# More matmuls on zeros at the start, and a shorter ScalarE program behind the last branch, in an attention and two-expert-layer kernel

## The chip, the cores and the metric

The kernel runs on one core of a Trainium2 chip, in one launch. The time is the device time of that launch in microseconds, from a handful of runs, of which the median counts. One further execution was profiled; its trace has a span (from the first to the last instruction) and the program's own time, which is a little longer.

The core has five engines that run side by side, each with its own instruction stream: TensorE (PE, with its weight loads as PEld), VectorE (DVE), ScalarE (ACT), GpSimd (POOL) and SyncE (SP, which here mostly issues DMA transfers).

## The reference, cut to what matters

Three layers follow each other. All is fp32; q, k, p are drawn eight times larger than the usual 0.1.

```python
# attention through 32 packed queries per head: q, k, v are (4, 8, 576, 64), p is (4, 8, 32, 64)
def sm_attn(qq, kk, vv):
    s = scale * qq @ kk.T;  a = exp(s - max(s));  a = a / (sum(a) + 1e-9);  return a @ vv
p_packed = sm_attn(p, k, v)
x = sm_attn(q, p_packed, p_packed)          # -> (2304, 512)

# first mixture: top-1 expert of 8 with a capacity of 2 * 2304 / 8 tokens
logits = x @ w_gate;  e = argmax(logits);  g = softmax(logits)[e]
keep a token while its expert has had fewer than `capacity`
x = g * (relu(x @ w1[e]) @ w2[e])           # w1 (8, 512, 1024), w2 (8, 1024, 512); zero where not kept

# second mixture: top-1 expert of 8, no capacity, and a sigmoid output gate
e = argmax(x @ w_gate2)
out = softmax(x @ w_gate2)[e] * sigmoid(x @ w_output_gate)[e] * (relu(x @ w1b[e]) @ w2b[e])
```

## The kernel before

The work is done per batch of 576 tokens. All four batches go through the attention; then the kernel looks at which experts the tokens chose and computes, as "slots", only those pairs of batch and expert that hold kept tokens. With the inputs given, two slots are enough. They are written out straight. What other inputs could need (two more slots, and a general path that loops over all experts) stands behind branches at the very end: `rest` is read from memory into a register of every engine (`values_load`, L1101), and `tc.If(rest > 0)` (L1102) skips all of it where nothing is left. With these inputs it is skipped: each engine reads the flag, takes the branch, and goes on to the waits that end the program (shown under L1102 and L1139, the line of `moe.close()` being the last of the function).

Matrix products in fp32 precision are made from split operands: a rounded copy "h" (ScalarE, a `Copy` or `Relu` activation) and the remainder "l" (VectorE, sometimes GpSimd), and three products hh, hl, lh. The functions `high`, `x_high`, `moe1_ppw`, `layer1`, `y_out`, `g2_l` and `moe2_layer2` each hold one such ScalarE instruction.

The order of the work up to the end of the first slot is written out by hand in `PLAN`: a list of steps that are recorded one after the other, each putting its instructions at the end of the streams of the engines it uses. `k00` loads the first third of batch 0's k (one DMA on SP's queue), `tk00` transposes that third on TensorE (six 128x128 transposes, tile `tp`, L25) and copies the result out of PSUM on ScalarE (tile `T`, L265), `p0`/`dup0`/`pT0` do the same for p, `sa00` makes the first scores (tile `s`), and `warm9` issues nine matmuls of a 128x256 block of zeros (`wz`, cleared by VectorE's first instruction, L103), whose result nobody reads:

```python
def warm(n):
    ps = psm("warm")
    for _ in range(n):
        mm(nc, ps[:, 0, 0:256], wz[:, 0:128], wz, True, True)
```

`psm` hands out the four PSUM tiles in turn; a tile is written again when its last reader four tiles earlier is done. The kernel's last useful instructions are in `moe2_layer2` with `last=True`: the last 128 rows of output are made in two halves of 256 columns, each scaled on ScalarE (L751) and sent by a DMA that ScalarE itself issues (L752).

Of the kernel before, what the change touches and what calls it, by code (L numbers as in the profile page):

```python
# [12 lines left out]
ACTF = mybir.ActivationFunctionType  # L13
ALU = mybir.AluOpType
# [11 lines left out]


PLAN = """
k00 hn0 tk00 k01 tk01 warm9 p0 dup0 k10 k02 tk10 tk02 pT0 k11 tk11 k12 p1 v00 q00 q01 tk12 sa00 k20 sa01 dup1 pT1 sa10
sa11 ma00 ea00 cst0 ma01 ea01 ma10 q02 dup2 ma11 cst1 warm7 ea10 at00D v01 at01D ea11 rs1 cap tq00 v02 tq01 tq02 k21  # L30
k22 pp00 v11 pp01 rs0 sc0A tk20 pT2 pt0 tk21 dup3 sb01 tr01 sb00 mb01 tk22 v12 at10 at11 tr00 su01 eb01 mb00 sa20 ma20
sa21 v10 gg0 v22 q10 sm01 q11 pp10 pp11 sc1 ea20 q12 su00 eb00 sm00 tq10 k32 k30 pt1A mu01 v32 tq11 tq12 pT3 warm4
ma21 k31 ea21 bk01 mu00 sb11 q20 bk00 lg01 tr11 mb11 at20D xh0 su11 at21 lt01 tk30 q21 tk31 tk32 eb11 oa01 ob0 rk01
kp01 q22 v20 v21 sb10 tr10 q30 tq20 q31 cn01 tq21 tq22 ei sm11 mu11 rs2 pp20 pp21 wa00 mb10 wa01 wa03 sa30 gg1 sa31
ma30 sc2A v31 pt2 ea30 ma31 tq30 ea31 v30 bk11 sb21 tr21 xl0 mb21 su21 at30 su10 tq31 at31D gg2 w00 sb20 tr20 mb20 w01
h01 q32 eb21 sm21 wb00 rs3 mu21 h00 su20 h03 pp30 eb10 wb01 sm10 pp31 sc3A w03 bk21 mu10 bk10 tq32 pt3A h02 sb30 tr30
sb31 tr31 mb31 wa02 cst3 cl wh00 h06 w02 wl00 eb20 sm20 gg3 mb30 su31 eb31 h07 wh01 sm31 mu20 wb03 bk20 y000 y001 wb02
su30 mu31 eb30 sm30 bk31 h04 h05 y002 y010 y011 y012 mu30 bk30 lg14 cr y013 wl01 lt14 wh03 y003 y004 y005 y006 oa14D
ob1 rk14 wh02 wl02D y014 y015 cst2 kp14 cn14 rt si wl03D y020 wa11 y007 prep y021 y030 wa10 y016 y022 y023 y024 yo00
wa13 y025 y026 y027 wb10 y017 yo01 y031 yo02 y032 y033 y034 xh1 xl1D y035 rr w11 w10 wb11 wa12 y036 y037 yo03 hn1 h13  # L40
zo3 h12 wh10 wl10D h11 h10 w13 w12 gl0 wb12 h14 wh12 gt h17 h15 wh11 wl11 h16 wb13 wh13 wl13D gs gi wl12D zo2
"""


# [1 line left out]
def tile_kernel(  # L46
# [16 lines left out]
    nc = tc.nc  # L63
# [33 lines left out]
        return ps_p.tile([128, 2, 512], FP32, tag="ps", name=name)  # L97

    dma_in = nc.sync.dma_start


    wz = const.tile([128, 256], BF16, name="wz")
# [444 lines left out]
    def high(src, nm, i):  # L547

        hi = (mp["ws2"] if i == 3 else mp["ws"]).tile([128, 1024], FP32R, tag="w", name=nm + "h")
        nc.scalar.activation(out=hi, in_=src.rearrange("p a b -> p (a b)"), func=ACTF.Copy)  # L550
        return hi.rearrange("p (a b) -> p a b", a=src.shape[1])

    def low(src, hi, nm, i, eng):
# [11 lines left out]
    def half(ap):  # L565
        return ap.rearrange("p (u n) -> p u n", u=2)
# [26 lines left out]

    def x_high(a2):
        xh = xs_p.tile([128, 2, S], FP32R, tag="xh", name="xh")
        nc.scalar.activation(out=xh, in_=a2, func=ACTF.Copy)
        return xh

    def x_low(a2, xh, eng):
# [17 lines left out]
    def moe1_ppw(pt, w):  # L617
        ps = ppw_mm(pt, w)
        wh = ppw_p.tile([128, 2, 256], FP32R, tag="wh", name="wh")
        wl = ppw_p.tile([128, 2, 256], FP32R, tag="wl", name="wl")  # L620
        nc.scalar.activation(out=wh, in_=ps[:, :, 0:256], func=ACTF.Copy)
        nc.vector.tensor_tensor(wl, ps[:, :, 0:256], wh.bitcast(FP32), op=ALU.subtract)
        return wh, wl

# [6 lines left out]
    def layer1(h, f, w, x, n, last_first=False):  # L631

        ps = psm("h")
        fs = slice((f % 2) * 128, (f % 2) * 128 + 128)
        chain(ps, [(w[i][:, c, fs], x[j][:, c, :]) for c in range(n) for i, j in ((0, 0), (0, 1), (1, 0))])
        hi = half(h[0][:, f, :])
        nc.scalar.activation(out=hi, in_=ps[:, :, 0:HS], func=ACTF.Relu)  # L637
        lo = h[1][:, f, :]
        cut = HS - LAST
        parts = [(half(lo), ps[:, :, 0:HS], hi)] if not last_first else [  # L640
            (lo[:, 0:HS], ps[:, 0, 0:HS], hi[:, 0]), (lo[:, HS:], ps[:, 1, 0:cut], hi[:, 1, 0:cut]),
            (h[2][:, f, S:S + LAST], ps[:, 1, cut:HS], hi[:, 1, cut:])]
        for o, i, a in parts:
            nc.vector.scalar_tensor_tensor(o, i, 0.0, a.bitcast(FP32), op0=ALU.max, op1=ALU.subtract)  # L644
# [7 lines left out]
                   kk == 0 and x == 0, kk == NF - 1 and x == 2)  # L652

    def y_out(ps, c, y):
        nc.scalar.activation(out=half(y[0][:, c, :]), in_=ps[:, :, 0:HS], func=ACTF.Copy)  # L655
        nc.vector.tensor_tensor(
            half(y[1][:, c, :]), ps[:, :, 0:HS], half(y[0][:, c, :]).bitcast(FP32), op=ALU.subtract)

# [10 lines left out]
    def g2_l(y):  # L669

        lp = psm("l2")
        chain(lp, [(wg2s[:, c, :], y[j][:, c, :]) for c in range(NC) for j in range(2)])
        nc.scalar.activation(out=half(lgT[:4 * E, 0:S]), in_=lp[:4 * E, :, 0:HS], func=ACTF.Copy)

    def g2_t(g1s, slot):
        tp = psm("lt2")
# [56 lines left out]
    def moe2_layer2(h, ws, t, g2, bsel, last=False):  # L733

        n = 128 if t < NT - 1 else LAST
        cs = slice(t * 128, t * 128 + n)
        ps = psm("o")
        o = mp["o"].tile([128, DM], FP32, tag="osb", name="osb")
        parts = ((0, 0), (1, 0), (0, 1))
        if n > 64:  # L740

            w = DM // 2 if last else DM
            seq = [(kk, i, j) for kk in range(NF) for i, j in parts]
            for u in range(DM // w):
                ds_ = slice(u * w, u * w + w)
                if u == 1:
                    ps = psm("o")
                for x, (kk, i, j) in enumerate(seq):
                    mm(nc, ps[:n, 0, 0:w], h[i][:, kk, cs], ws[kk // 2][j][:, kk % 2, ds_], x == 0, x == len(seq) - 1)
                if last:  # L750
                    nc.scalar.activation(out=o[:n, ds_], in_=ps[:n, 0, 0:w], func=ACTF.Copy, scale=g2[:n, t:t + 1])  # L751
                    nc.scalar.dma_start(  # L752
                        out.rearrange("(b s) d -> b s d", b=B)[bass.ds(bsel, 1), t * 128:t * 128 + n, ds_].rearrange(
                            "o s d -> (o s) d"), o[:n, ds_])
            if last:
                return
            nc.scalar.activation(out=o[:n], in_=ps[:n, 0, :], func=ACTF.Copy, scale=g2[:n, t:t + 1])  # L757
        else:
            for kk in range(NF):
                for j in range(2):  # L760
                    mm(nc, ps[:2 * n, 0, :], h[2][:, kk, S - n:S + n], ws[kk // 2][j][:, kk % 2, :],
                       kk == 0 and j == 0, kk == NF - 1 and j == 1)
            nc.scalar.activation(out=o[:n], in_=ps[n:2 * n, 0, :], func=ACTF.Copy)
            nc.vector.tensor_tensor(o[:n], o[:n], ps[:n, 0, :], op=ALU.add)  # L764
            nc.gpsimd.tensor_scalar(o[:n], o[:n], g2[:n, t:t + 1], None, op0=ALU.mult)  # L765
        nc.sync.dma_start(
            out.rearrange("(b s) d -> b s d", b=B)[bass.ds(bsel, 1), t * 128:t * 128 + n, :].rearrange(
                "o s d -> (o s) d"), o[:n])
# [74 lines left out]
    def general():  # L843
# [46 lines left out]
        def relu1(h, f, w, x, n):  # L890
            ps = psm("h")
            fs = slice((f % 2) * 128, (f % 2) * 128 + 128)
            chain(ps, [(w[:, c, fs], x[:, c, :]) for c in range(n)])
            nc.scalar.activation(out=half(h[:, f, :]), in_=ps[:, :, 0:HS], func=ACTF.Relu)

        for b in range(B):
            nc.vector.memset(yacc[b], 0.0)
# [1 line left out]
        with tc.For_i(0, E, 1) as e:  # L899
# [3 lines left out]
            for b in range(B):  # L903
# [4 lines left out]
                for f in range(NF):  # L908
                    if f % 2 == 0:
                        ps = ppw_mm(ppT[:, b], w1s[f // 2])  # L910
                        w = ppw_p.tile([128, 2, 256], FP32, tag="wh", name="wf")
                        nc.scalar.activation(out=w, in_=ps[:, :, 0:256], func=ACTF.Copy)
                    relu1(h, f, w, am, 2)
                for c in range(NC):
                    ps = psm("y")
# [2 lines left out]
                    nc.vector.tensor_tensor(ya, ya, ps[:, :, 0:HS], op=ALU.add)  # L918
        for b in range(B):
            y = new_h()[0:2]  # L920
            nc.scalar.activation(out=y[0][:, 0:NC], in_=yacc[b], func=ACTF.Copy)
            nc.vector.tensor_tensor(y[1][:, 0:NC], yacc[b], y[0][:, 0:NC].bitcast(FP32), op=ALU.subtract)
            g2_l(y)
            K16, oel = g2_t(g1[:, b], b)
            nc.vector.tensor_copy(K2all[:, b * NT:(b + 1) * NT], K16)
            nc.vector.tensor_copy(g2all[:, b * NT:(b + 1) * NT], g2_g(oel, g1[:, b], f"g{b}"))
# [34 lines left out]
    with tc.manual_schedule():  # L961
# [136 lines left out]
        for t in order:  # L1098
            last = t == order[-1]
            moe2_layer2(h, ws, t, g2_1, bs1_act if last else bs1, last)  # L1100
    rest = nc.values_load(flag_i[0:1, 1:2], min_val=0, max_val=3 * B)  # L1101
    with tc.If(rest > 0):  # L1102
        slots_left = nc.values_load(flag_i[0:1, 0:1], min_val=0, max_val=1)
        with tc.If(slots_left > 0):
# [39 lines left out]
```

## Time and profile before

| | |
|---|---|
| median of 3 runs | 251.66 us (250.22 to 253.41) |
| profiled execution, its own time | 250.77 us |
| its span, first to last instruction | 249.0 us |
| TensorE busy | 237.3 us (95% of the span) |
| VectorE / ScalarE / GpSimd busy | 123.7 / 102.3 / 37.7 us |
| DMA | 37.14 MB, mean 149 GB/s |

Busy time is what the engines spent in work; branches, register loads, waits on semaphores and the issuing of DMA are not counted in it, so that the end of the program, which consists of them, shows as idle in such a table and has to be read from the rows of those instructions. A row that names an engine with a q (ACTq, SPq) is such an instruction. "PEclk" is the granted clock of TensorE as a share of its higher level, 2.4 GHz; 0.5 is the lower one, 1.2 GHz. The records of it in this trace begin at 7.2 us; the column shows 1.00 before that, so that the clock of the first microseconds has to be read from how long like instructions take.

### The profile page before, as it was taken

How to read it: one execution, taken by the hardware profiler on the slowest of the kernel's cores; microseconds unless marked ns; L12 is line 12 of the kernel's file. 1: busy time of each engine (PE TensorE's matmuls, PEld its weight loads, DVE VectorE, ACT ScalarE, POOL GpSimd, SP SyncE). 2: the span in 40 equal slices, each digit the busy share in tenths (PEclk: the TensorE clock that was granted, in tenths of full speed). 3: DMA queues.
4: the chain of work that ended last, by engine and by line, in shares of the span. 5: the costliest groups of instructions: out<-in, count | busy, mean ns of one | idle time of the engine just before them, and what ended most of it. 6: DMA issues, size and time to landing. Idle time of an engine off the chain costs nothing.

```text
span 249.0 us, 5609 instructions
## 1 busy us (share of the span) xinstructions
PE 237.3 (95%) x2297; PEld 213.5 (86%) x2297; DVE 123.7 (50%) x313; ACT 102.3 (41%) x160; POOL 37.7 (15%) x65
## 2 busy tenths in 40 slices
PE   3899999899999999999999999999999999999991
PEld 3668877688979998899999999998888999988891
DVE  0063989899958747757533524880310526611000
ACT  2667887866631143654122522641221514511110
POOL 6011633635750000003000000000200000002000
PEclk9999999999999999999999999999999999999997
DMA  6999897993300197990472240073011730001211
GB/s 221 378 338 334 282 339 259 322 355 109 87 3 0 47 304 216 301 294 17 141 212 79 83 164 0 0 245 114 31 55 45 230 152 3 1 0 43 67 56 38
DMA packets 33474, 37.14 MB, mean 149 GB/s; under 512 B 5280, under 2 KB 27168, under 8 KB 33440
## 3 DMA queue, kind: packets, MB, share of 16 engines
q1 hardware_dynamic: 33152, 36.43, 45.2%
q8 instruction: 20, 0.33, 0.5%
q10 hardware_dynamic: 288, 0.26, 0.3%
q14 instruction: 14, 0.11, 0.2%
HBM read 31.25 MB, written 4.72 MB: 144 GB/s over the span
## 4 chain that ended last, share of the span: by engine, by line
PE 89%; DMA 3%; DVE 2%; ACT 2%; issue 1%; SPq 1%; ACTq 0%
PE h L21 31%; PE y L21 21%; PE o L21 21%; PE tp L25 4%; PE s L21 3%; DMA r<-in_k_dram 3%; PE a1Tp L25 2%; PE l L21 2%; PE ppw L21 2%; PE pp L21 2%; ACT T L265 1%; PE lp L21 1%; PE lt L25 1%; SPq L304 1%; PE warm L21 0%
## 5 line engine op out<-in xcount | busy, mean ns | idle before, releaser
L21 PE MATMUL o<-w2bh,h 128*128 128x512 f32 (+1 forms) x160 | 46.7, 369 | 0.0
L21 PE MATMUL y<-h,w2ah 128*128 128x288 f32 x256 | 44.9, 297 | 0.0
L644 DVE SCALAR_TENSOR_TENSOR h<-h 128x576 fp32r<-128x576 f32 (+3 forms) x64 | 26.1, 450 | 26.1 <-ACT h L637 26.1
L21 PEld LDWEIGHTS y<-h,w2ah 128*128 128x128 f32 x256 | 37.5, 189 | 0.9 <-issue 0.9
L637 ACT ACTIVATE h<-h 128x576 fp32r<-128x576 f32 x32 | 20.8, 650 | 36.7 <-PE h L21 34.1
L21 PEld LDWEIGHTS o<-w2bh,h 128*128 128x128 f32 x160 | 28.9, 188 | 5.2
L21 PE MATMUL o<-w2bl,h 128*128 128x512 f32 (+1 forms) x88 | 32.6, 371 | 0.0
L21 PE MATMUL h<-yh,w1bh 128*128 128x288 f32 x128 | 27.5, 296 | 0.0
L21 PE MATMUL y<-h,w2al 128*128 128x288 f32 x128 | 27.4, 296 | 0.0
L21 PE MATMUL h<-yh,w1bl 128*128 128x288 f32 x128 | 27.4, 295 | 0.0
L21 PE MATMUL h<-yl,w1bh 128*128 128x288 f32 x128 | 27.3, 295 | 0.0
L25 PE MATMUL tp<-ident,r 128*128 128x128 f32 x144 | 20.4, 288 | 5.0 <-DMA r<-in_k_dram 4.8
L25 PEld LDWEIGHTS tp<-ident,r 128*128 128x128 f32 x144 | 16.8, 148 | 7.6 <-POOL revv L119 4.2
L265 ACT ACTIVATE T<-tp 128x768 f32<-128x768 f32 x24 | 19.6, 850 | 8.9 <-PE tp L25 8.5
L21 PEld LDWEIGHTS h<-yh,w1bh 128*128 128x128 f32 x128 | 20.6, 189 | 0.2
L21 PEld LDWEIGHTS h<-yh,w1bl 128*128 128x128 f32 x128 | 20.6, 188 | 0.0
L21 PEld LDWEIGHTS y<-h,w2al 128*128 128x128 f32 x128 | 20.6, 188 | 0.0
L21 PEld LDWEIGHTS h<-yl,w1bh 128*128 128x128 f32 x128 | 20.6, 188 | 0.0
L765 POOL TENSOR_SCALAR osb<-osb,g 64x512 f32<-64x512 f32 x2 | 3.2, 1578 | 111.5 <-DVE osb L764 111.5
L21 PEld LDWEIGHTS o<-w2bl,h 128*128 128x128 f32 x88 | 16.5, 188 | 2.9
L655 ACT ACTIVATE yh<-y 128x576 fp32r<-128x576 f32 x8 | 5.1, 652 | 31.5 <-PE y L21 31.5
L757 ACT ACTIVATE osb<-o,g 128x512 f32<-128x512 f32 x7 | 4.8, 690 | 32.0 <-PE o L21 24.2
(176 smaller groups left out, 344.2 us busy)
## 6 DMA issues: line engine op xcount, KB each, us to landing
wraw<-in_moe_w_dram SPq DMA_DIRECT2D x32, 512.0 KB, 5.0
r<-in_k_dram SPq DMA_DIRECT2D x12, 384.0 KB, 6.5
r<-in_q_dram SPq DMA_DIRECT2D x12, 384.0 KB, 6.8
v<-in_v_dram SPq DMA_DIRECT2D x8, 512.0 KB, 7.3
out_dram<-zt SPq DMA_DIRECT2D x2, 1152.0 KB, 7.9
out_dram<-osb SPq DMA_DIRECT2D x7, 256.0 KB, 2.1
a2s<-a2T SPq DMA_DIRECT2D x1, 576.0 KB, 5.5
v<-in_v_dram SPq DMA_DIRECT2D x4, 128.0 KB, 5.3
```

What stands on the lines that cost most here:

```text
L21: return nc.tensor.matmul(out, lhsT=lhsT, rhs=rhs, start=start, stop=stop)
L25: return nc.tensor.transpose(out, in_, ident)
L265: nc.scalar.activation(out=o, in_=i, func=ACTF.Copy)
L304: dma_in(t, (k if nm == "k" else q)[b].rearrange("h (x r) d -> (h x) r d", r=R)[:, 2 * PJ * a:2 * PJ * (a + 1), :])
L637: nc.scalar.activation(out=hi, in_=ps[:, :, 0:HS], func=ACTF.Relu)
L644: nc.vector.scalar_tensor_tensor(o, i, 0.0, a.bitcast(FP32), op0=ALU.max, op1=ALU.subtract)
L655: nc.scalar.activation(out=half(y[0][:, c, :]), in_=ps[:, :, 0:HS], func=ACTF.Copy)
L757: nc.scalar.activation(out=o[:n], in_=ps[:n, 0, :], func=ACTF.Copy, scale=g2[:n, t:t + 1])
L765: nc.gpsimd.tensor_scalar(o[:n], o[:n], g2[:n, t:t + 1], None, op0=ALU.mult)
```

## The change

Two edits that do not touch each other.

1. `PLAN` begins with two more steps, `warm9 warm6`: fifteen more matmuls on zeros, ahead of everything else. The rest of the list is the same.
2. A helper `scopy` takes the place of the direct ScalarE activations in the functions named above. While `skipped[0]` is False it issues the same activation as before. Just before `tc.If(rest > 0)` it is set to True, so that the code recorded behind the branch gets VectorE instructions in their place. What is left of ScalarE there are the exponentials.

```diff
 PLAN = """
-k00 hn0 tk00 k01 tk01 warm9 p0 dup0 k10 k02 tk10 tk02 pT0 ...
+warm9 warm6 k00 hn0 tk00 k01 tk01 warm9 p0 dup0 k10 k02 tk10 tk02 pT0 ...
...
+    skipped = [False]
+
+    def scopy(out, in_, func=ACTF.Copy, scale=1.0):
+        if not skipped[0]:
+            nc.scalar.activation(out=out, in_=in_, func=func, scale=scale)
+        elif func == ACTF.Relu:
+            nc.vector.tensor_scalar(out, in_, 0.0, None, op0=ALU.max)
+        elif isinstance(scale, float):
+            nc.vector.tensor_copy(out, in_)
+        else:
+            nc.vector.tensor_scalar(out, in_, scale, None, op0=ALU.mult)
...
-        nc.scalar.activation(out=hi, in_=ps[:, :, 0:HS], func=ACTF.Relu)
+        scopy(hi, ps[:, :, 0:HS], ACTF.Relu)
...
-            nc.scalar.activation(out=o[:n], in_=ps[:n, 0, :], func=ACTF.Copy, scale=g2[:n, t:t + 1])
+            scopy(o[:n], ps[:n, 0, :], scale=g2[:n, t:t + 1])
...
     rest = nc.values_load(flag_i[0:1, 1:2], min_val=0, max_val=3 * B)
+    skipped[0] = True
     with tc.If(rest > 0):
```

TensorE's program, at its very start (`tp` are the transposes of `tk00` and `tk01`, `wz` and `warm` the zeros). Before:

```order
L1139 UNCONDITIONAL_BRANCH
L25 MATMUL tp<-ident,r 128x128 x12
L21 LDWEIGHTS wz
L21 MATMUL warm<-wz 128x256
...
L25 MATMUL tp<-ident,r 128x128 x12
L25 MATMUL pTp<-ident,p_sb 128x128 x2
```

and now, with fifteen pairs of the zeros ahead of the first transposes, and nine behind them as before:

```order
L1154 UNCONDITIONAL_BRANCH
L21 LDWEIGHTS wz
L21 MATMUL warm<-wz 128x256
...
L21 LDWEIGHTS wz
L21 MATMUL warm<-wz 128x256
L25 MATMUL tp<-ident,r 128x128 x12
L21 LDWEIGHTS wz
L21 MATMUL warm<-wz 128x256
...
L25 MATMUL tp<-ident,r 128x128 x12
```

Nothing else of TensorE's stream changes its place ahead of the last branch.

ScalarE's program, from its last DMA over the last branch (L1102 before, L1117 now; `flag_i` is the flag, `osb` the last output). Before:

```order
L752 DMA out_dram<-osb 128x256
L1101 TENSOR_LOAD flag_i
L1102 COMPARE_AND_BRANCH
L1103 TENSOR_LOAD flag_i
L1104 COMPARE_AND_BRANCH
L596 ACTIVATE xh<-a2s 128x1152
L621 ACTIVATE wh<-ppw 128x512
L637 ACTIVATE h<-h 128x576 x2
L550 ACTIVATE w2ah<-wraw 128x1024
```

and now:

```order
L766 DMA out_dram<-osb 128x256
L1115 TENSOR_LOAD flag_i
L1117 COMPARE_AND_BRANCH
L1118 TENSOR_LOAD flag_i
L1119 COMPARE_AND_BRANCH
L218 ACTIVATE d<-d 128x40
L721 ACTIVATE zs<-zs 128x5
L218 ACTIVATE d<-d 128x40
L721 ACTIVATE zs<-zs 128x5
L1119 UNCONDITIONAL_BRANCH x2
```

In all, 210 operations of ScalarE stood behind that branch, 186 of them ACTIVATE; now there are 36, with 12 ACTIVATE. (Register moves and pure waits are not in these counts.) On VectorE the count behind the branch rises from 404 to 578; on GpSimd it is 35, on SP 194 and on TensorE 2410, before and now.

## Rows read from the trace of the kernel before

**Rows 1.** The page: engine busy times; DMA share in 40 slices; instruction fetch queue (packets, MB).

```profile
PE 237.3 (95%) x2297; PEld 213.5 (86%) x2297; DVE 123.7 (50%) x313; ACT 102.3 (41%) x160; POOL 37.7 (15%) x65
DMA  6999897993300197990472240073011730001211
q14 instruction: 14, 0.11, 0.2%
```

**Rows 2.** Chain of work that ended last: start us, us, what.

```profile
2.67 6.79 DMA r<-in_k_dram
9.60 0.86 PE tp L25 x6
...
12.47 1.13 PE s L21 x32
...
243.88 0.47 ACT osb L751
```

**Rows 3.** TensorE's timeline, 4 to 16 us: start, us, what [idle before <-releaser].

```profile
4.24 2.79 PE L25 MATMUL tp<-ident,r 128*128 128x128 f32 x12 [4.24 <-DMA r<-in_k_dram]
6.82 1.35 PE L21 MATMUL warm<-wz 128*128 128x256 bf16 x9
8.55 0.88 PE L25 MATMUL tp<-ident,r 128*128 128x128 f32 x6 [0.38 <-DMA r<-in_k_dram]
...
14.51 1.20 PE L21 MATMUL s<-T,pT 64*32 64x288 f32 x32 [0.54 <-ACT pT L332]
```

**Rows 4.** The same timeline, 7.24 to 8.2 us: the zeros after the first.

```profile
7.04 1.14 PE L21 MATMUL warm<-wz 128*128 128x256 bf16 x8
```

**Rows 5.** ScalarE's timeline, 8 to 16 us, first row.

```profile
9.46 0.81 ACT L265 ACTIVATE T<-tp 128x768 f32<-128x768 f32 x1 [1.59 <-PE tp L25]
```

**Rows 6.** Windows: stretch, us, busy PE PEld DVE ACT POOL, PEclk, DMA share, GB/s.

```profile
4.20:7.20 3.00, 2.96 (x14) 2.85 (x15) 0.00 (x0) 0.95 (x2) 0.56 (x2) 1.00 1.02 337
...
246.10:249.00 2.90, 0.00 (x0) 0.00 (x0) 0.00 (x0) 0.00 (x0) 0.00 (x0) 0.51 0.05 11
```

**Rows 7.** Line L1102, the branch: count, duration ns min/median/max, first and last start.

```profile
L1102 SPq EVENT_SEMAPHORE  x9: 17/17/17, 242.2 to 246.5; - x9
L1102 POOLq EVENT_SEMAPHORE  x2: 17/17/17, 230.3 to 230.4; - x2
L1102 DVEq EVENT_SEMAPHORE  x2: 21/21/21, 231.5 to 231.7; - x2
L1102 PEldq EVENT_SEMAPHORE  x2: 51/51/51, 245.6 to 245.8; - x2
L1102 ACTq EVENT_SEMAPHORE  x2: 17/17/17, 247.8 to 247.9; - x2
L1102 DVEq COMPARE_BRANCH  x1: 72/72/72, 228.5 to 228.5; - x1
L1102 POOLq COMPARE_BRANCH  x1: 45/45/45, 229.2 to 229.2; - x1
...
L1102 PEldq COMPARE_BRANCH  x1: 3438/3438/3438, 242.2 to 242.2; - x1
L1102 ACTq COMPARE_BRANCH  x1: 54/54/54, 245.1 to 245.1; - x1
```

**Rows 8.** Line L1139, the closing waits of SP, same columns.

```profile
L1139 SPq EVENT_SEMAPHORE  x10: 17/28/1096, 246.6 to 248.9; - x10
```

**Rows 9.** SP's own waits, 245 to 250 us: us in total, times, longest.

```profile
SPq L1139 <- ACTq L1102: 1.1, 1, 1.1
```

**Rows 10.** GpSimd's last work, timeline.

```profile
228.66 1.57 POOL L765 TENSOR_SCALAR osb<-osb,g 64x512 f32<-64x512 f32 x1 [49.56 <-DVE osb L764]
```

**Rows 11.** DMA of 228 to 230.1 us: packets, MB, share.

```profile
q14 instruction: 1, 0.01, 1.6%
```

**Rows 12.** DMA of 245.2 to 248 us.

```profile
q14 instruction: 1, 0.01, 0.8%
```

**Rows 13.** VectorE's first instruction, timeline.

```profile
0.91 0.17 DVE L103 MEMSET wz<- 128x128 uint32 x1 [0.91 <-PEq L1128]
```

More of the change, by code (lines that the diff above doesn't have):

```diff
@@ L28 @@
 PLAN = """
[L29 to L38, printed above, removed]
@@ L39 @@
-ob1 rk14 wh02 wl02D y014 y015 cst2 kp14 cn14 rt si wl03D y020 wa11 y007 prep y021 y030 wa10 y016 y022 y023 y024 yo00
-wa13 y025 y026 y027 wb10 y017 yo01 y031 yo02 y032 y033 y034 xh1 xl1D y035 rr w11 w10 wb11 wa12 y036 y037 yo03 hn1 h13
-zo3 h12 wh10 wl10D h11 h10 w13 w12 gl0 wb12 h14 wh12 gt h17 h15 wh11 wl11 h16 wb13 wh13 wl13D gs gi wl12D zo2
+warm9 warm6 k00 hn0 tk00 k01 tk01 warm9 p0 dup0 k10 k02 tk10 tk02 pT0 k11 tk11 k12 p1 v00 q00 q01 tk12 sa00 k20 sa01
+dup1 pT1 sa10 sa11 ma00 ea00 cst0 ma01 ea01 ma10 q02 dup2 ma11 cst1 warm7 ea10 at00D v01 at01D ea11 rs1 cap tq00 v02
@@ new lines @@
+tq01 tq02 k21 k22 pp00 v11 pp01 rs0 sc0A tk20 pT2 pt0 tk21 dup3 sb01 tr01 sb00 mb01 tk22 v12 at10 at11 tr00 su01 eb01
+mb00 sa20 ma20 sa21 v10 gg0 v22 q10 sm01 q11 pp10 pp11 sc1 ea20 q12 su00 eb00 sm00 tq10 k32 k30 pt1A mu01 v32 tq11
+tq12 pT3 warm4 ma21 k31 ea21 bk01 mu00 sb11 q20 bk00 lg01 tr11 mb11 at20D xh0 su11 at21 lt01 tk30 q21 tk31 tk32 eb11
+oa01 ob0 rk01 kp01 q22 v20 v21 sb10 tr10 q30 tq20 q31 cn01 tq21 tq22 ei sm11 mu11 rs2 pp20 pp21 wa00 mb10 wa01 wa03
+sa30 gg1 sa31 ma30 sc2A v31 pt2 ea30 ma31 tq30 ea31 v30 bk11 sb21 tr21 xl0 mb21 su21 at30 su10 tq31 at31D gg2 w00 sb20
@@ new lines @@
+tr20 mb20 w01 h01 q32 eb21 sm21 wb00 rs3 mu21 h00 su20 h03 pp30 eb10 wb01 sm10 pp31 sc3A w03 bk21 mu10 bk10 tq32 pt3A
+h02 sb30 tr30 sb31 tr31 mb31 wa02 cst3 cl wh00 h06 w02 wl00 eb20 sm20 gg3 mb30 su31 eb31 h07 wh01 sm31 mu20 wb03 bk20
+y000 y001 wb02 su30 mu31 eb30 sm30 bk31 h04 h05 y002 y010 y011 y012 mu30 bk30 lg14 cr y013 wl01 lt14 wh03 y003 y004
+y005 y006 oa14D ob1 rk14 wh02 wl02D y014 y015 cst2 kp14 cn14 rt si wl03D y020 wa11 y007 prep y021 y030 wa10 y016 y022
+y023 y024 yo00 wa13 y025 y026 y027 wb10 y017 yo01 y031 yo02 y032 y033 y034 xh1 xl1D y035 rr w11 w10 wb11 wa12 y036
@@ L42 @@
+y037 yo03 hn1 h13 zo3 h12 wh10 wl10D h11 h10 w13 w12 gl0 wb12 h14 wh12 gt h17 h15 wh11 wl11 h16 wb13 wh13 wl13D gs gi
+wl12D zo2
 """
@@ L549, in high @@
         hi = (mp["ws2"] if i == 3 else mp["ws"]).tile([128, 1024], FP32R, tag="w", name=nm + "h")
-        nc.scalar.activation(out=hi, in_=src.rearrange("p a b -> p (a b)"), func=ACTF.Copy)
+        scopy(hi, src.rearrange("p a b -> p (a b)"))
         return hi.rearrange("p (a b) -> p a b", a=src.shape[1])
@@ L595, in x_high @@
         xh = xs_p.tile([128, 2, S], FP32R, tag="xh", name="xh")
-        nc.scalar.activation(out=xh, in_=a2, func=ACTF.Copy)
+        scopy(xh, a2)
         return xh
@@ L620, in moe1_ppw @@
         wl = ppw_p.tile([128, 2, 256], FP32R, tag="wl", name="wl")
-        nc.scalar.activation(out=wh, in_=ps[:, :, 0:256], func=ACTF.Copy)
+        scopy(wh, ps[:, :, 0:256])
         nc.vector.tensor_tensor(wl, ps[:, :, 0:256], wh.bitcast(FP32), op=ALU.subtract)
@@ L654, in y_out @@
     def y_out(ps, c, y):
-        nc.scalar.activation(out=half(y[0][:, c, :]), in_=ps[:, :, 0:HS], func=ACTF.Copy)
+        scopy(half(y[0][:, c, :]), ps[:, :, 0:HS])
         nc.vector.tensor_tensor(
@@ L672, in g2_l @@
         chain(lp, [(wg2s[:, c, :], y[j][:, c, :]) for c in range(NC) for j in range(2)])
-        nc.scalar.activation(out=half(lgT[:4 * E, 0:S]), in_=lp[:4 * E, :, 0:HS], func=ACTF.Copy)
+        scopy(half(lgT[:4 * E, 0:S]), lp[:4 * E, :, 0:HS])
     def g2_t(g1s, slot):
@@ L762, in moe2_layer2 @@
                        kk == 0 and j == 0, kk == NF - 1 and j == 1)
-            nc.scalar.activation(out=o[:n], in_=ps[n:2 * n, 0, :], func=ACTF.Copy)
+            scopy(o[:n], ps[n:2 * n, 0, :])
             nc.vector.tensor_tensor(o[:n], o[:n], ps[:n, 0, :], op=ALU.add)
@@ L893, in relu1 @@
             chain(ps, [(w[:, c, fs], x[:, c, :]) for c in range(n)])
-            nc.scalar.activation(out=half(h[:, f, :]), in_=ps[:, :, 0:HS], func=ACTF.Relu)
+            scopy(half(h[:, f, :]), ps[:, :, 0:HS], ACTF.Relu)
         for b in range(B):
@@ L911, in general @@
                         w = ppw_p.tile([128, 2, 256], FP32, tag="wh", name="wf")
-                        nc.scalar.activation(out=w, in_=ps[:, :, 0:256], func=ACTF.Copy)
+                        scopy(w, ps[:, :, 0:256])
                     relu1(h, f, w, am, 2)
@@ L920, in general @@
             y = new_h()[0:2]
-            nc.scalar.activation(out=y[0][:, 0:NC], in_=yacc[b], func=ACTF.Copy)
+            scopy(y[0][:, 0:NC], yacc[b])
             nc.vector.tensor_tensor(y[1][:, 0:NC], yacc[b], y[0][:, 0:NC].bitcast(FP32), op=ALU.subtract)
```

## The prediction

> **What bounds the kernel now.** I read the busy times first: TensorE works 237.3 of 249.0 us [rows 1], so the time is TensorE's work plus what lies before its first and behind its last instruction. The two edits touch just these ends, so next come the chain of waits and the timelines there.
>
> At the start the chain is a transfer: k's third piece, from 2.67 to 9.46 us, and TensorE takes it up at 9.60 [rows 2]. TensorE starts at 4.24 when the first k arrives, makes twelve transposes in 2.79 us, then nine matmuls on zeros, and at 8.55 waits again for k, as the releaser in the brackets says [rows 3]. The six transposes there take 0.88 us, though half of twelve at the first rate would be 1.40 [rows 3]. The zeros show where that changed: the first began at 6.82, the second at 7.04, 0.22 us later, and the eight from there took 1.14 together [rows 3, 4]. So TensorE was at its lower level, 1.2 GHz, from 4.24 to about 7.1, and at 2.4 GHz from then on. It had been busy for 2.96 of the 3.00 us ahead of that [rows 6].
>
> At the end TensorE's last result is copied out from 243.88 to 244.35 by ScalarE [rows 2], which then issues the last DMA. Nothing is counted as busy for the 4.6 us that are left, so the rows of the branch and of the closing waits must be read. The branch shows for each engine when it jumped and when its next instruction ran [rows 7]: VectorE 228.5 to 231.5, TensorE 242.2 to 245.6, ScalarE 245.1 to 247.8, GpSimd 229.2 to 230.3. GpSimd's gap is not the branch's: its own 1.57 us operation began at 228.66 and ended at 230.23 [rows 10], and the next instruction ran at 230.3. SP is through with the landings of the DMAs at 246.5 [rows 7], goes into its closing waits at 246.6, and the longest of these lasts 1096 ns [rows 8]; the wait list names ScalarE at L1102 for it, 1.1 us [rows 9]. So ScalarE's late return from its jump is the last thing that ends, by 1.1 us.
>
> **What the long jump is.** GpSimd skips 35 listed operations, ScalarE 210, SP 194, VectorE 404, TensorE 2410. The four with many lose 2.6 to 3.4 us each, the one with 35 nothing that shows. In the stretch in which both VectorE and GpSimd jump there is one packet of the instruction queue [rows 11], so only one of the two loaded code, and that must be VectorE, whose gap is 3.0 us. In ScalarE's gap there is one such packet too [rows 12]. I read it as this: a far target has to be loaded first, a near one is there already.
>
> A rule of the Trainium skill (the page "Runtime: NRT & Kernel Launch", section "Instruction fetch mechanics") says the same of a taken branch, that its target is fetched when it lies outside the two blocks that the engine holds. By the block that the Trainium skill gives there, 256 instructions, ScalarE's present jump would mostly end within what is held, its 2.6 us would be something else, and this part of the change would be worth nothing. The packets of that queue are 0.11 MB / 14 = 8 KB in this trace [rows 1]. That is half of the block in the Trainium skill, and the trace decides; the case is still kept as the first rival.
>
> **Part one, the fifteen matmuls on zeros.** They need only VectorE's first memset, so they can run while TensorE stands idle, up to 4.24 [rows 3]. Price of one: 0.22 us at the lower level (above), 1.14 / 8 = 0.14 at the higher [rows 4]; fifteen are 2.1 to 3.3 us. With the memset done at 1.08 us [rows 13] they end between 3.2 and 4.4. At worst the first transposes begin 0.2 us late. Before, TensorE rose after some 3 us of work that began at 4.24; now that work begins at 1.1, so I expect the twelve transposes at the higher level: two sixes at 0.88 are 1.76 instead of 2.79 us, 1.03 less [rows 3].
>
> None of it reaches the end. ScalarE, which copies these transposes out, is idle for 1.59 us before its copy at 9.46 [rows 5], TensorE waits for k at 8.55 and takes up the piece that the chain shows at 9.60 [rows 2, 3], and the DMA engines are 90% busy or more in the second to the fourth slice, 6 to 25 us [rows 1], so the pieces come no sooner. If all twelve ran late instead, by 0.2 us, the same idle time hides that. The cover is the transfer: were k there at once, the 1.03 us would count. Worth: 0, with bounds of -1.03 (it carries through) and +1.5 (second rival).
>
> The two more PSUM tiles only move the turn of the four buffers by two; each still waits for the reader four tiles earlier. Price 0.
>
> **Part two, ScalarE's shorter program.** Up to the branch ScalarE issues the same instructions; price 0. Behind it 36 listed operations are left, against GpSimd's 35, so I take GpSimd's row as the nearest: no load, and the next instruction within about 0.1 us of the jump. ScalarE would run on at 245.3 instead of 247.8. What is late next is SP itself, at 246.5 with the last landing, and TensorE's row at 245.8 [rows 7] is earlier than that. So SP's long wait of 1096 ns shrinks to the 28 ns of its neighbours [rows 8]: **-1.07 us**. Of the 2.5 us that ScalarE wins, the other 1.4 are worth nothing. The bounds are 0 (the load stays) and -1.07 (SP's landings cap it).
>
> VectorE has 174 operations more behind the branch. They aren't run. Its jump loads code already and is over at 231.5 to 231.7, 15 us ahead of the end [rows 7]; even one more load of 3 us is hidden there. Price 0. SP, GpSimd and TensorE skip as much as before.
>
> **The sum.** 250.77 (the profiled execution's own time; 1.77 of it lie outside the span) - 0 - 1.07 = 249.70. The median of the runs shown is 0.89 above that execution, so the forecast for a median is 251.66 - 1.07 = 250.6.
>
> **Rivals.**
>
> *The jump stays long* (chance 0.12): 36 operations are still too far, since register moves and waits come on top and the target may lie across a block's end, or the gap is no code load at all. For: no row shows ScalarE with a short jump. Against: GpSimd's 35. Time 251.7, no change.
>
> *The clock falls back, slower than before* (0.15). If the twelve transposes end near 5.8 and the nine zeros near 7.0, TensorE stands idle until k comes at 8.55: about 1.6 us where it was 0.38 [rows 3]. The trace shows it keep the higher level through 0.54 us of idling [rows 3], and shows it lose it once: in the last stretch, from 246.10, the granted clock is 0.51, and TensorE's work had ended about 243.9 [rows 2, 6], 2.2 us earlier. The new gap lies between, and the point that decides is whether it is long enough to be taken for idleness. If so, the transposes and scores from 8.55 on run at 1.2 GHz, and I take for the length of it the 3.0 us that the lower level lasted at the start [rows 6]; they lie on the chain [rows 2], and at half speed 3.0 us of time hold 1.5 us less of work. 250.6 + 1.5 = 252.1, slower by 0.4.
>
> *The start carries through* (0.08): the pieces of k come earlier than TensorE needs them in most runs, and the profiled one was unlucky. Then 1.03 more is won: 249.6. Against it stand two waits for k in one head.
>
> **How the numbers follow.** The forecast has 0.65. Its own spread is that of medians of a few runs which lie between 250.22 and 253.41, some 1.3 us to either side: 249.3 to 251.9. The range takes in the slower rival and the faster one with part of that spread, 248.8 to 252.5. A difference of 2% is 5.0 us, about what a measurement of this kernel can tell from no change. No case comes near it: faster by more 0.02, slower by more 0.03, for something not on this list, such as a wait moved somewhere in the 200 us that I call untouched; within 2%: 0.95.
>
> **What would show it.** In the profile after: fifteen zeros ending by 4.4; the first twelve transposes in about 1.8 us; TensorE still waiting for k near 8.5 and 9.6, the six there in 0.88 (1.4 would be the clock rival). At the end: ScalarE's next instruction within 0.2 us of its jump and no packet of the instruction queue between; SP's longest closing wait gone, and some 1.8 us, not 2.85, from the last landing to the end. A ScalarE gap of 2.6 us or a new wait of SP for TensorE or VectorE would prove the second part wrong; a chain that begins with transposes instead of the transfer of k, the first.

## The result and the profile after

The changed kernel takes 249.59 us in the median of 12 runs (248.67 to 250.63), the kernel before 251.62 us beside it (250.22 to 253.98): a ratio of 0.992, 95% interval 0.990 to 0.994, or -2.0 us. It is inside the range, and the sign is the one forecast, but the size is about twice the -1.07 us of the sum. The end won what was forecast; the fifteen pairs on zeros won some 0.6 to 1.1 us that had been priced at nothing, and not for the reason that any of my cases gave.

The end first. ScalarE's last copy, and the end of the span, in the profile after (a timeline row: start, us, what):

```profile
243.36 0.47 ACT L765 ACTIVATE osb<-o,g 128x256 f32<-128x256 f32 x1 [2.33 <-PE o L21]
```

The span is 247.4 us, so 4.0 us follow that copy's start, where it was 5.1 (249.0 - 243.88) before [rows 2]. The rows of the branch (now L1117) and of the closing waits (now L1154), same columns as [rows 7, 8]:

```profile
L1117 SPq EVENT_SEMAPHORE  x9: 17/17/17, 241.8 to 246.0; - x9
...
L1117 DVEq EVENT_SEMAPHORE  x2: 21/21/21, 230.8 to 231.0; - x2
L1117 ACTq EVENT_SEMAPHORE  x2: 17/17/17, 244.8 to 244.9; - x2
L1117 PEldq EVENT_SEMAPHORE  x2: 51/51/51, 245.6 to 245.7; - x2
...
L1117 ACTq COMPARE_BRANCH  x1: 54/54/54, 244.6 to 244.6; - x1
```

```profile
L1154 SPq EVENT_SEMAPHORE  x10: 17/28/28, 246.1 to 247.3; - x10
```

ScalarE runs on 0.2 us after its jump, not 2.6. The longest of SP's closing waits is 28 ns, not 1096. SP's waits name ScalarE no more (compare [rows 9]); the 0.6 us for TensorE stood in the profile of before too:

```profile
SPq L1117 <- SPq L1117: 3.8, 2, 2.6
SPq L1154 <- PEq L1154: 0.6, 2, 0.4
```

The DMA queues of 244.6 to 247 us hold no packet of q14, the instruction queue that ScalarE's code comes on, where [rows 12] had one; the packet of q8, which carries 16 KB packets, is TensorE's:

```profile
q10 hardware_dynamic: 144, 0.13, 16.4%
q8 instruction: 1, 0.02, 2.4%
```

The start, in TensorE's timeline after (compare [rows 3]):

```profile
1.13 3.26 PE L21 MATMUL warm<-wz 128*128 128x256 bf16 x15 [1.13 <-DVE wz L117]
4.22 1.80 PE L25 MATMUL tp<-ident,r 128*128 128x128 f32 x12
5.86 1.15 PE L21 MATMUL warm<-wz 128*128 128x256 bf16 x9
6.87 0.85 PE L25 MATMUL tp<-ident,r 128*128 128x128 f32 x6
7.92 0.85 PE L25 MATMUL tp<-ident,r 128*128 128x128 f32 x6 [0.20 <-DMA r<-in_k_dram]
```

The zeros end by 4.4 and the twelve transposes take 1.80 us, both as forecast. But the next six begin at 6.87, with no wait for k, 1.7 us sooner than before. That looked like my third rival, which gave 249.6: k comes earlier than in the one profile of before, and TensorE was what the start waited for. I took it for the explanation (theory S below: the time at the start is TensorE's, not the transfer's), and it was wrong.

### The profile page after: what moved, and what is told of

It is laid out like the page before. It is cut to its first block, busy times and chain, and to the rows that moved or that the text cites. A ratio compares the mean times of both kernels' runs of the same rounds, so it can differ in the third digit from the quotient of the medians.

```text
span 247.4 us, 5640 instructions
## 1 busy us (share of the span) xinstructions
PE 239.5 (97%) x2312; PEld 214.7 (87%) x2312; DVE 123.7 (50%) x313; ACT 102.3 (41%) x160; POOL 37.6 (15%) x65
## 4 chain that ended last, share of the span: by engine, by line
PE 86%; DMA 9%; ACT 2%; SPq 1%; issue 1%; DVE 0%; ACTq 0%
PE h L21 31%; PE y L21 21%; PE o L21 21%; DMA v<-in_v_dram 4%; DMA r<-in_q_dram 3%; PE tp L25 3%; DMA r<-in_k_dram 2%; PE l L21 2%; PE s L21 2%; PE pp L21 2%; PE ppw L21 2%; ACT T L279 1%; PE a1Tp L25 1%; PE lp L21 1%; SPq L318 1%; PE lt L25 1%
## 5 line engine op out<-in xcount | busy, mean ns | idle before, releaser
L25 PE MATMUL tp<-ident,r 128*128 128x128 f32 x144 | 19.2, 276 | 0.7 <-DMA r<-in_k_dram 0.2
L25 PEld LDWEIGHTS tp<-ident,r 128*128 128x128 f32 x144 | 15.7, 141 | 3.6 <-ACT T L279 1.2
```

What stands on the lines that cost most here:

```text
L25: return nc.tensor.transpose(out, in_, ident)
```

## The experiments

Ratios are to the kernel before, run on the same chip beside each.

**The two parts apart, the kernel before again, and thirty zeros.**

```diff
# zeros alone: the kernel before with
-k00 hn0 tk00 ...
+warm9 warm6 k00 hn0 tk00 ...
# shorter ScalarE program alone: the changed kernel with
-warm9 warm6 k00 hn0 tk00 ...
+k00 hn0 tk00 ...
# thirty zeros: the changed kernel with
-warm9 warm6 k00 hn0 tk00 ...
+warm9 warm9 warm9 warm3 k00 hn0 tk00 ...
```

> The kernel before with the fifteen zeros alone. Theory S (the start is TensorE's): in most executions k's third transfer lands at about 6.8 us, as in the profile after, and not at 8.5, as in the one profiled execution of before; then the twelve slow transposes and the nine zeros, which end at 8.17, hold the next transposes, and the zeros win what they save there, 1.0 us: ratio 0.996 (0.9945 to 0.9975). Rival T (the start is the transfer's, as the prediction had it): 0.0, ratio 1.000, and the whole difference is at the end. Both: ScalarE's jump at the end still takes 2.6 us and SP still waits 1.1 us for it.

Measured: 250.73 us, ratio 0.9978 (0.9951 to 1.0005): -0.6 us by the ratio, -1.1 by the medians (251.80 beside it). That lies between S and T, and the interval holds T's 1.000, so this run decides nothing by itself. ScalarE's jump still takes 2.8 us (244.8 to 247.6) and SP waits 1.3 us for it.

> The kernel before with the shorter ScalarE program behind the last branch alone. Theory S: -1.1 us, ratio 0.9956, and the first twelve transposes take 2.8 us as before. Rival T: the whole -2.0 us, ratio 0.992. Both: ScalarE runs on within 0.2 us of its jump and the instruction queue carries no packet in that time.

Measured: 250.59 us, ratio 0.9948 (0.9929 to 0.9967): -1.3 us, with the -1.07 inside. ScalarE's jump is at 245.2 and its next instruction at 245.4. The end is worth what the sum had, and the rest belongs to the fifteen pairs: the changed kernel stands 1.0 us below this one by the medians, 0.7 by the ratios.

> The kernel before, unchanged, for a second profile and for the spread of its times. Theory S: ratio 1.000 (0.997 to 1.003); in this profile k10's transposes begin right behind the nine zeros, at about 8.2 us, with no wait for a transfer, since k has landed by 7. Rival T: they wait for k again and begin near 8.5.

Measured: 251.81 us, ratio 0.9989 (0.9961 to 1.0017). k's third third is taken up at 8.10 with no wait for a transfer, as S said. What I had not looked for stands further on, in TensorE's timeline from 26 us, in the burst of eighty 32x64 matmuls that make `pp`:

```profile
26.95 0.30 PE L21 MATMUL pp<-v,a1T 128*32 128x64 f32 x4
27.83 1.36 PE L21 MATMUL pp<-v,a1T 128*32 128x64 f32 x76 [0.57 <-issue]
```

Four run, then TensorE stands for 0.57 us without a releaser ("issue": nothing in the profile that it waited for). The first profile of before and that of the shorter ScalarE program alone, with the same instructions ahead, show no such pause: one profile of three has it.

> The changed kernel with thirty zeros ahead of the first transposes in place of fifteen. They end some 1.6 us later (15 at 0.11 us), at about 6.0, and the first transposes with them. Theory S: TensorE is what the start waits for, so the third third of k is transposed at about 8.4 instead of 6.9, and the time is 1.0 to 1.5 us above that of the changed kernel, about that of the kernel with the shorter ScalarE program alone: ratio to before 0.996. Rival T: the transfer covers the delay, ratio as the changed kernel, 0.992.

Measured: 250.88 us, ratio 0.9960 (0.9936 to 0.9983), as S said. The last run below takes this support away again.

**Fewer zeros, and ScalarE's program half restored.**

```diff
# no inner zeros, and no zeros at all: the changed kernel with
-warm9 warm6 k00 hn0 tk00 k01 tk01 warm9 p0 ...
+warm9 warm6 k00 hn0 tk00 k01 tk01 p0 ...
+k00 hn0 tk00 k01 tk01 p0 ...
# slots on ScalarE: the changed kernel with
-    skipped[0] = True
     with tc.If(rest > 0):
...
+        skipped[0] = True
         with tc.If(mixed > 0):
             general()
```

> The changed kernel without the nine zeros between the first twelve transposes and k's third third. TensorE is then free from about 5.8 us until that third lands (6.7 to 7.2 in the profiles of the changed kernel and of the one with the zeros alone). Theory S: in the changed kernel these nine end at 6.84, just as the transfer does, so leaving them out wins at most 0.1 us: ratio to before 0.992, the same as the changed kernel. Rival F (the clock falls back in a gap of 1 to 1.5 us): the six transposes of k's third third take 1.4 us in place of 0.85 and the scores up to twice as long, 0.5 to 1.5 us lost: ratio 0.994 to 0.998.

Measured: 250.32 us, ratio 0.9951 (0.9918 to 0.9984). That is 0.7 above the changed kernel, which would be the loss of F; but in its profile the transposes behind a wait of 0.88 us ran at the higher clock:

```profile
1.13 3.38 PE L21 MATMUL warm<-wz 128*128 128x256 bf16 x15 [1.13 <-DVE wz L117]
4.40 2.72 PE L25 MATMUL tp<-ident,r 128*128 128x128 f32 x12
8.00 1.80 PE L25 MATMUL tp<-ident,r 128*128 128x128 f32 x12 [0.88 <-DMA r<-in_k_dram]
```

The twelve behind the wait take 1.80 us, the twelve ahead of it 2.72. These first twelve ran at the lower clock in spite of the fifteen zeros ahead of them, so the zeros do not even give the faster transposes in every execution.

> The changed kernel with ScalarE's copies put back in the two skipped slots, and on VectorE in the general path alone: about 130 listed operations of ScalarE behind the branch, between the 36 of the change and the 210 of before. Theory N (what counts is whether the target lies in the code that is held ahead, blocks of 8 KB, 128 instructions, of which the next is there): some 180 instructions with moves and waits end in the next block, ScalarE runs on within 0.2 us, ratio as the changed kernel, 0.992. Rival C (only a jump of a few dozen is near): a packet of the instruction queue follows the jump, ScalarE runs on 2.6 us later, SP waits 1.1 us, and the time is 1.1 us above the changed kernel: ratio 0.996.

Measured: 251.89 us, ratio 1.0005 (0.9974 to 1.0036). Neither had it. ScalarE ran on 0.5 us after its jump (245.0 to 245.5, with no packet of q14 between; 122 operations are listed for it behind the branches), so that its program is near enough, as N says. TensorE was late: between the two waits behind its jump and its drain, the next instruction of its program in the trace, lie 3.1 us:

```profile
L1116 PEldq EVENT_SEMAPHORE  x2: 51/51/51, 245.8 to 245.9; - x2
```

```profile
L1154 PEldq DRAIN  x2: 8/8/8, 249.0 to 249.4; - x2
```

and between the two the queues of 246 to 249 us hold a packet of TensorE's code:

```profile
q8 instruction: 1, 0.02, 2.2%
q14 instruction: 1, 0.01, 0.9%
```

SP waited 2.6 us for TensorE in place of the 0.6 of the changed kernel.

> The changed kernel with neither the fifteen zeros nor the nine: the first transposes run at the lower clock as before, and TensorE is free when they end, at 7.0. Theory S1 (what held k's third third in the kernel before was TensorE's queue, transposes and zeros together): without the nine zeros it begins when it lands, at about 7.1, still at the lower clock in part of the executions (six in up to 1.4 us): 0.2 to 0.8 us above the changed kernel, ratio to before 0.993 to 0.996. Theory S2 (it is the clock that counts, TensorE must be kept busy until it has risen): the clock rises late, the transposes and scores up to 10 us run at half rate, 1.0 to 2.0 us above the changed kernel, ratio 0.996 to 1.000. Rival T (the start is the transfer's): as the changed kernel, 0.992.

Measured: 252.11 us, ratio 1.0016 (0.9983 to 1.0049), 2.5 us above the changed kernel by the medians, and above S2's range, into which the interval reaches. But its profile's start is as good as the changed kernel's, with the first scores at 10.78 us against 10.71. The loss is the pause in the burst at 26 us again, now ten matmuls further into it and three times as long:

```profile
25.87 0.43 PE L21 MATMUL pp<-v,a1T 128*32 128x64 f32 x14
28.20 1.24 PE L21 MATMUL pp<-v,a1T 128*32 128x64 f32 x66 [1.90 <-issue]
```

This kernel has nine pairs of weight load and matmul less ahead of the burst than the kernel before, and its pause comes ten matmuls later in it: the pause keeps its place in the count of instructions. In both profiles 705 of TensorE's instructions (weight loads, matmuls and waits) stand ahead of it. TensorE's code comes in 16 KB packets; the last one ahead of the end of the pause landed at 26.68 us here and at 26.27 in the repeat of before, and TensorE ran on 1.5 and 1.6 us after it. So TensorE waited for code, the next block of its program. And the pause cost more than itself. The windows of this profile (columns as in [rows 6]):

```profile
25.60:29.30 3.70, 1.80 (x111) 1.45 (x89) 1.88 (x5) 1.78 (x4) 2.13 (x2) 1.00 0.78 300
29.30:32.80 3.50, 3.50 (x32) 3.43 (x17) 3.13 (x8) 1.29 (x3) 1.16 (x1) 0.51 0.55 123
```

The granted clock fell to its lower level behind it: six transposes at 29.37 took 1.54 us, where six at the higher level take 0.85.

**The same number of instructions without the work, and the reverse.** In place of zeros, `tiny` issues matmuls of one column.

```diff
+    def tiny(n):
+        ps = psm("warm")
+        for _ in range(n):
+            mm(nc, ps[:, 0, 0:1], wz[:, 0:128], wz[:, 0:1], True, True)
# fifteen tiny, thirty tiny
-warm9 warm6 k00 hn0 tk00 k01 tk01 warm9 ...
+tiny9 tiny6 k00 hn0 tk00 k01 tk01 warm9 ...
+tiny9 tiny9 tiny9 tiny3 k00 hn0 tk00 k01 tk01 warm9 ...
# no zeros, same count; and the kernel without zeros, the same placed late
+tiny9 tiny9 tiny6 k00 hn0 tk00 k01 tk01 p0 ...
-... pT3 warm4 ma21 ...
+... pT3 warm4 tiny9 tiny9 tiny6 ma21 ...
# slots on ScalarE, moved
-... pT3 warm4 ma21 ...
+... pT3 warm8 ma21 ...
```

> The changed kernel with the fifteen matmuls on zeros cut from 256 columns to one: as many instructions of TensorE, so that every later instruction has the same place in its code blocks, but work for a fraction of the time, over by 2.5 us. Theory S (the zeros help by what the clock and the first transposes win): the first twelve transposes take 2.8 us as before and the next begin at 8.1 or later, ratio to before as the shorter ScalarE program alone, 0.995. Rival A (the fifteen pairs help by moving the rest of TensorE's code against its 16 KB blocks): ratio as the changed kernel, 0.992.

Measured: 249.31 us, ratio 0.9917 (0.9885 to 0.9949), the changed kernel's. S's 0.995 lies just outside the interval. The start of its profile has all that S called the loss, and none of it showed in the time:

```profile
1.13 0.56 PE L21 MATMUL warm<-wz 128*128 128x1 bf16 x15 [1.13 <-DVE wz L117]
4.42 2.79 PE L25 MATMUL tp<-ident,r 128*128 128x128 f32 x12 [2.73 <-POOL lgT L189]
7.01 1.80 PE L21 MATMUL warm<-wz 128*128 128x256 bf16 x9
8.64 1.47 PE L25 MATMUL tp<-ident,r 128*128 128x128 f32 x12
```

> The kernel without any zeros ahead of k's third third, which took 252.11 us, with twenty-four matmuls of one column at the very start in their place: as many instructions of TensorE as the changed kernel has. Rival A (that kernel lost 2.5 us because its code blocks ended elsewhere, in a burst of short matmuls at 26 us where TensorE stood for 1.9 us without a releaser): the pause is gone, 0.2 to 0.8 us above the changed kernel, ratio to before 0.993 to 0.996. Theory S2 (it lost them by the clock): 252.1 us again, ratio 1.000 to 1.002.

Measured: 249.67 us, ratio 0.9926 (0.9898 to 0.9955): 2.4 us won back by twenty-four matmuls of one column. The burst runs through:

```profile
26.97 1.39 PE L21 MATMUL pp<-v,a1T 128*32 128x64 f32 x80
```

> The kernel with ScalarE's copies left in the skipped slots, in which TensorE, not ScalarE, was late at the very end (its last waits at 245.9, its drain at 249.0, a packet of its instruction queue between), with four more zeros in an existing step at 33 us, so that TensorE's target lies eight instructions further. Theory N (a code block's end lay between these two instructions; ScalarE's jump of some 130 listed operations is near enough): TensorE's drain follows its waits at once, SP's wait for it is gone, 0 to 0.4 us above the changed kernel, ratio to before 0.992 to 0.994. Rival C (such a ScalarE program is slow in itself): the 249.0 stays, ratio 1.000.

Measured: 249.80 us, ratio 0.9923 (0.9896 to 0.9949). Four matmuls of no use (their step runs at 31 us in this profile, not 33) won 2.1 us, since TensorE's drain now follows its waits at 244.9 and 245.0:

```profile
L1154 PEldq DRAIN  x2: 8/8/8, 245.2 to 246.6; - x2
```

So in these runs a jump (ScalarE's 2.6 us before) or a step (TensorE's 3.1 us) into code that is not there yet cost a load.

> The kernel without any zeros ahead of k's third third (252.11 us), with the twenty-four matmuls of one column behind the zeros at 33 us and not at the start: the same instructions in all as in the run with them at the start (249.67 us), but up to 33 us each stands where it stood in the slow kernel. Theory A (the place of the code blocks' ends in the bursts before 33 us decides): TensorE again stands without a releaser in the burst of 32x64 matmuls near 26 us until the next block has landed, 252 to 253 us, ratio to before 1.000 to 1.006. Rival B (it is the extra matmuls or the places at the end of the program): 249.7 to 250.3, ratio 0.992 to 0.995.

Measured: 251.97 us, ratio 1.0017 (0.9985 to 1.0049). The same twenty-four matmuls behind the burst win nothing, and the pause is where it was, after the fourteenth and behind 705 instructions:

```profile
26.35 0.43 PE L21 MATMUL pp<-v,a1T 128*32 128x64 f32 x14
28.30 1.24 PE L21 MATMUL pp<-v,a1T 128*32 128x64 f32 x66 [1.52 <-issue]
```

> The changed kernel with thirty matmuls of one column for its fifteen zeros: the code is moved as in the run with thirty zeros (250.88 us), but the first transposes are not held up. If that run lost its 1.3 us against the changed kernel by the late transposes: 249.3 to 249.8, ratio to before 0.990 to 0.993. If it lost them by the places of the blocks' ends: 250.6 to 251, ratio 0.996.

Measured: 250.78 us, ratio 0.9980 (0.9953 to 1.0006). With the code moved as in the run with thirty zeros the time is that run's (250.88), though the first transposes begin at 4.18 and not at 6.86. So 2.7 us of delay at the start cost nothing that can be measured, and what that run lost goes with the count of its instructions. The profile of thirty tiny shows no pause of the matmuls. That of the thirty zeros shows one, behind 961 instructions, which is 256 further than 705, and 1.4 us after the next packet had landed (30.00 us):

```profile
31.39 0.27 PE L25 MATMUL tp<-ident,r 128*128 128x128 f32 x1 [0.32 <-issue]
```

That profile also has a wait of 0.49 us for weights at 104 us. How much of the 1.2 us that these two kernels lose to the changed one comes from such places isn't shown.

All runs with the short ScalarE program and an untouched end, by how many pairs TensorE has ahead of the burst at 26 us, against the kernel before:

| pairs | what stands there | median us | ratio to before |
|---|---|---|---|
| -9 | no zeros; the same, tiny ones placed late | 252.11; 251.97 | 1.0016; 1.0017 |
| 0 | zeros as before | 250.59 | 0.9948 |
| +6 | fifteen zeros, inner nine left out | 250.32 | 0.9951 |
| +15 | fifteen zeros; fifteen tiny; twenty-four tiny and no zeros | 249.59; 249.31; 249.67 | 0.9918; 0.9917; 0.9926 |
| +30 | thirty zeros; thirty tiny | 250.88; 250.78 | 0.9960; 0.9980 |

The time goes with the row, not with what stands in it. But a row fixes more than the place of the code. Each step of zeros or tiny also takes one of the four PSUM tiles, and the kernels of a row stand at the same turn of them: one step back, 0, one, two and four steps on, so that +30 has the turn of row 0, and nearly its time. No run separates the two. For the code speak the pauses behind 705 and 961 instructions, each of which ended 1.4 to 1.6 us after a packet landed; against the turn, that a tile waits for the reader four tiles earlier whatever the turn, and that no wait of TensorE above 0.15 us from 14 us on goes with it in the profiles. For the step from 0 to +15, the change itself, the code is therefore the likely cause and not a shown one.

No run beats the changed kernel by more than 0.3 us in the median.

## Why the prediction was right, and where it was not

**ScalarE's jump, -1.07: right, in mechanism and size.** That part alone gave 0.9948 (-1.3 us, interval -1.8 to -0.8), SP's long wait went, the 1.4 us beyond SP's own landings were worth nothing, and the reading of GpSimd's row as the near case held. The first rival, that the jump stays long, is out. The distance that is near enough is larger than the 36 operations: with the slots' copies on ScalarE (122 operations) it still ran on in 0.5 us.

**"None of it reaches the end", of the clock and the transposes: right.** In the profile after TensorE was not even waiting for the piece of k that the sentence rested on; but the cover is real, and wider than I knew. The chain of waits of that profile still begins with transfers, of k, q and v, up to the burst at 26 us, and not with transposes (columns as in [rows 2]):

```profile
3.15 5.61 DMA r<-in_k_dram
8.78 8.00 DMA r<-in_q_dram
16.79 9.19 DMA v<-in_v_dram
26.11 1.37 PE pp L21 x80
```

With fifteen matmuls of one column, and the transposes at the lower clock, the first scores begin 0.9 us later (11.58 for 10.71) but the burst only 0.45 (26.56 for 26.11), and the time was the changed kernel's. Transposes 2.7 us later in the pair with thirty gave the same time too.

**The step that failed: part one, "Worth: 0".** I costed the fifteen pairs by their time on TensorE and by the PSUM tiles, and left out that thirty instructions move all later ones against the blocks in which TensorE's code is loaded. I had used such loads to explain the jumps, and did not ask of them anywhere else. The term is -0.7 us by the ratios (0.9918 / 0.9948) and -1.0 by the medians; the zeros alone gave -0.6 and -1.1. That it comes from the instructions and not from their work is shown: fifteen matmuls of one column won the same. That it comes through the code blocks is inferred. In the burst at 26 us the block's end stands after four matmuls in the kernel before; fifteen pairs more put it ahead of the burst. In the profiled execution of before the block came in time, so its rows could not show a pause, and its time lay 0.9 below the median, which I noted without asking what it might lack. That a typical execution of before pauses there isn't shown: one profile of three with that place of the code has 0.57 us, and kernels with the block's end elsewhere win or lose. How the 0.6 to 1.1 us split over this and other blocks isn't shown either.

**The clock rival: the mechanism exists, not here.** TensorE's gap before k was 0 to 0.2 us in the profile after. In the kernel without zeros a pause of 1.90 us was followed by a granted clock of 0.51 (29.3 to 32.8 us). The pause of 1.52 us with tiny ones placed late was not (1.00 from 28.3 to 36 us), and neither was a wait of 0.95 us with the slots on ScalarE, where twelve transposes take 1.77 us ahead of it and 1.82 behind:

```profile
7.86 1.82 PE L25 MATMUL tp<-ident,r 128*128 128x128 f32 x12 [0.95 <-DMA r<-in_k_dram]
```

**The third rival gave 249.6 by the wrong road.** A number that fits is no evidence for its mechanism: only the matmuls of one column, which have the count without the work, told them apart. And 249.59 lies inside the range because the range allowed for the scatter of medians and for that rival; the sum has only half of the change, so the hit is in part luck.

## What to carry to other kernels

An edit that adds or removes instructions of an engine moves all that follow against the blocks in which its code is loaded; where short instructions come in bursts (the 1.90 us at 26 us), or a jump lands (the 3.1 us at the end), that can outweigh what the instructions do. Before believing that filler work helped, run the same count of instructions with no work in them. And code that is skipped is not free: what stands behind an untaken path sets how far the jump goes, so keep it short on the engine that ends last.

## What the runs showed of the hardware that was not expected

- TensorE can wait for code in the middle of straight-line work: 0.57, 1.52 and 1.90 us in the burst of 160 instructions in 1.4 us, and 0.32 us once at 31 us, each ending 1.4 to 1.6 us after a packet of its code had landed. The Trainium skill ("Runtime: NRT & Kernel Launch", "Instruction fetch mechanics") holds that crossing a 16 KB boundary is mostly hidden. The size agrees here (0.33 MB in 20 packets). The hiding holds at most block ends of these traces and not at those named. If the block before began 256 listed instructions ahead of the 705, the packet for the burst started 4.9 to 6.0 us after TensorE had entered that block in the three profiles with a pause there, and 2.2 to 4.0 us after it in those without; what sets that delay is open.
- Code that ran over a block's end right behind a jump's target paid twice: 3.1 us between two of TensorE's closing instructions, besides the jump's own load.
- TensorE at work on zeros from 1.13 us got its higher clock at about 4.1 us in the profile after and near 6.9 in the one without the inner zeros, where the trace's records of the clock begin: the same twelve transposes took 1.80 and 2.72 us.
